# Pairs of neighbouring feature blocks, and w_in loaded by halves of its rows

## The chip, the cores and the metric

The kernel runs on one core of a Trainium2 chip. TensorE (PE in the profile) multiplies matrices, VectorE (DVE) and GpSimd (POOL) do elementwise work, ScalarE (ACT) applies functions, SyncE (SP) issues the transfers, and 16 DMA engines carry them. The metric is the time of the device from start to end in microseconds. Before the change it is 690.95 us, the median of 3 runs (690.75 to 691.02).

## The reference

Two blocks follow each other. The first is a linear attention with decay, for 4 batches and 8 heads, over 768 positions with 64 channels per head. The second takes its output as 3072 tokens of 512 features and applies two weight matrices with a leaky rectifier between them.

```python
for b in range(nb):                                   # blocks of 64 positions
    intra = einsum('bhic,bhjc->bhij', qb, kb) * Dmask
    intra = einsum('bhij,bhjd->bhid', intra, vb)
    inter = einsum('bhid,bhde->bhie', qb * lam_pow, kv_state)
    out[:, :, sl] = intra + inter
    kv_state = lam_block * kv_state + einsum('bhsd,bhse->bhde', kb * rev_pow, vb)
# ...
x = out.transpose(0, 2, 1, 3).reshape(3072, 512)
h = x @ w_in                                          # w_in: 512 x 2048
g = maximum(0.01 * h, h)
return (g @ w_out).astype(float32)                    # w_out: 2048 x 512
```

The inputs w_in and w_out are 8-byte floating-point numbers (8 bytes per element, 8 MB each), while q, k, v and the output are float32. All arithmetic on the chip is in float32.

## The kernel before

**Loading.** Each matrix of weights comes in 16 loads of 512 KB. Blocks are named (kind, p, h): kind is `wi` or `wo`, p is one of 8 pairs, h is the first or second half of the pair. The 2048 hidden features are cut in 16 blocks of 128. Before the change, pair p is made of the feature blocks p and p + 8 (`f = p + NP * h`, NP = 8):

```python
blocks = [(w, p, h) for u in range(NU) for w in ("wi", "wo") for p in range(UP * u, UP * u + UP) for h in range(2)]
# ...
def load_w(n):
    w, p, h = blocks[n]
    f = p + NP * h
    rooms[n] = room_free(n)
    # ... t is a staging room; some rooms are tiles of later weights
    def go():
        if w == "wi":
            nc.sync.dma_start(out=w_raw[n].rearrange("p (ko f) -> p ko f", ko=KO), in_=w_in_r[:, :, f * P:(f + 1) * P])
        else:
            nc.sync.dma_start(out=w_raw[n], in_=moe_w_out[f * P:(f + 1) * P, :])
```

A row of w_in is 16 KB, and a load of w_in takes 128 columns of all 512 rows: 512 pieces of 128 x 8 bytes = 1 KB. A load of w_out takes 128 whole rows of 4 KB.

**Conversion.** [...]each number is made into a float32 from its two 32-bit words. ScalarE makes the magnitude of the high word (L273), the low part (L284) and the sign (L287), for each half h. VectorE clamps (L292) and shifts (L296) the whole pair, and adds the low part for each half (L301).

```python
def dest():
    return W[p][:, 0:4:3, :] if (kind == "wi") == (h == 0) else W[p][:, 1:3, :]
def words(i, dt):
    return w_raw[n].bitcast(dt).rearrange("p (n two) -> p n two", two=2)[:, :, i].rearrange("p (a b) -> p a b", a=2)
# ...
nc.scalar.activation(out=dest(), in_=words(1, F32), func=AF.Abs)                                   # L273
nc.scalar.activation(out=addend(U16, 0), in_=words(0, U32), func=AF.Copy, bias=0.0, scale=2.0 ** -29)   # L284
nc.scalar.activation(out=addend(BF16, 1), in_=words(1, F32), func=AF.Sign, bias=tiny[:, 0:1])      # L287
# ...
nc.vector.tensor_scalar(d, d, HI_MIN, HI_MAX, op0=ALU.max, op1=ALU.min)                            # L292
nc.vector.tensor_scalar(d, d, 3, None, op0=ALU.logical_shift_left)                                 # L296
nc.vector.tensor_tensor(d, d, lo.pop(n).rearrange("p (a b) -> p a b", a=2), op=ALU.add)            # L301
```

**Seven products for eight.** Both multiplications treat their operands as 2 x 2 blocks and use seven products of sums of blocks in place of eight products of blocks. For the weights, four differences are formed per pair by three subtractions (L308), on VectorE for the pairs listed in `T_DVE` and on GpSimd for the others: a wide one gives T1 and T3 side by side, then come T2 and T4, which takes the place of B12. Pairs are counted in the order of loading (wi0, wi1, wo0, wo1, wi2, wi3, ...), so pair 3 is wo1 and pair 4 is wi2. `SI` and `SO` say at which place of a weight tile each block stands, for w_in and w_out.

```python
PROD = {"P1": ("A11", "B11"), "P2": ("A12", "B21"), "P3": ("S4", "B22"), "P4": ("A22", "T4"),
        "P5": ("S1", "T1"), "P6": ("S2", "T2"), "P7": ("S3", "T3")}
eng, e = ("DVE", nc.vector) if n // 2 in T_DVE else ("POOL", nc.gpsimd)
for o, x, y, m in (("T1", "B12", "B11", 2), ("T2", "B22", "T1", 1), ("T4", "B21", "T2", 1)):
    later[eng + " T"].append((yes, us, part(o, x, y, m), [("w", n)], (o, n)))
```

The products are issued in the order P1, P2, P6, P5, P7, P3, P4. One product is 8 matmuls of 128x128 by 128x256. There are 6 groups of tokens (GC = 4 chunks of 128 tokens each), 4 units of weights, and an `up` (L587, with w_in) and a `down` (L613, with w_out) for each. The sums S1 to S4 of the left operand are formed at L558: `xs` from the attention's output, `gS` and two more from the rectified features. The 24 chunks of the attention are done in three parts each (transposes of k and q at L370, scores and states at L354, the output at L354), placed between the products.

**The order.** A small model in the kernel's own text decides where on each engine an instruction is issued. Its settings are the string of loads (`c` is q, k and v of one chunk, `w` one load of weights), the look-ahead of the loads, `T_DVE`, and the number of attention parts beside each group of products (`STEPS`).

```python
LOADS = "cwcwcwwcwwwwcwwwcccwcwwcwwwwwwwwwwwwwwwwww" + "c" * NCH
SLACK, AHEAD = (0.7, 0), (10.0, 16.0)
T_DVE = [0, 3, 7, 9, 11, 13, 14, 15]
FIRST, STEPS = 2, [2, 2, 1, 5, 5, 6, 3, 3, 0, 0, 0, 3, 0, 1, 0, 4]
```

The transfers all stand in one queue in SyncE's order. Each waits for the transfer eight places ahead of it to have landed, besides its own room being free.

Of the kernel before, what the change touches and what calls it, by code (L numbers as in the profile page):

```python
# [38 lines left out]
F32 = mybir.dt.float32  # L39
# [5 lines left out]
ALU = mybir.AluOpType  # L45
AF = mybir.ActivationFunctionType
# [13 lines left out]
def kernel(  # L60
# [10 lines left out]
    nc = tc.nc  # L71
    P = 128
# [6 lines left out]
    KO = d_model // P  # L79
    FO = d_ff // P  # L80
    NCH = B * NCB
# [3 lines left out]
    NP = FO // 2  # L85
    HD = d_model // 2
    UP = 2
# [57 lines left out]


    QB = 2 * P
    SI = {"B11": 0, "T4": 1, "B22": 2, "B21": 3, "T1": 4, "T3": 5, "T2": 6, "B12": 1}
    SO = {"B21": 0, "B11": 1, "T4": 2, "B22": 3, "T1": 4, "T3": 5, "T2": 6, "B12": 2}
    WI, WO = [None] * NP, [None] * NP  # L150
    w_in_r = moe_w_in.rearrange("(ko ki) n -> ki ko n", ki=P)


    blocks = [(w, p, h) for u in range(NU) for w in ("wi", "wo") for p in range(UP * u, UP * u + UP) for h in range(2)]
# [2 lines left out]
    ROOMS = ["st"] + [f"{w}{p}" for w, p, h in reversed(blocks) if h == 0 and p >= UP]  # L157


    LOADS = "cwcwcwwcwwwwcwwwcccwcwwcwwwwwwwwwwwwwwwwww" + "c" * NCH  # L160
    SLACK, AHEAD = (0.7, 0), (10.0, 16.0)

    T_DVE = [0, 3, 7, 9, 11, 13, 14, 15]

    FIRST, STEPS = 2, [2, 2, 1, 5, 5, 6, 3, 3, 0, 0, 0, 3, 0, 1, 0, 4]
    rooms = {}
    w_raw, lo, w_done = {}, {}, 0

# [50 lines left out]

    def load_w(n):  # L220
        w, p, h = blocks[n]
        f = p + NP * h
        rooms[n] = room_free(n)
        pool, size = (tp, 2 * d_model) if rooms[n] == "st" else (wop, 7 * QB)
        t = pool.tile([P, size], F32, name="ws", tag=rooms[n], bufs=1)
        w_raw[n] = t[:, 0:2 * d_model].bitcast(I64)

        def go():
            if w == "wi":
                nc.sync.dma_start(out=w_raw[n].rearrange("p (ko f) -> p ko f", ko=KO), in_=w_in_r[:, :, f * P:(f + 1) * P])  # L230
            else:
                nc.sync.dma_start(out=w_raw[n], in_=moe_w_out[f * P:(f + 1) * P, :])

        run("DMA", 1.95, go, [("lowp", m) for m in range(n) if rooms[m] == rooms[n]], ("raw", n))
        ready["raw", n] += 2.0

    def room_free(n):
        later_on = {f"{w}{p}" for w, p, h in blocks[n + 1:] if (w, p) != blocks[n][:2]} | {"st"}
        return next((r for r in ROOMS if r in later_on and r not in taken()), None)

    def taken():
        return {rooms[m] for m in w_raw}
# [4 lines left out]
    def conversion(n, first):  # L247

        kind, p, h = blocks[n]
        W, s = (WI, SI) if kind == "wi" else (WO, SO)

        def dest():
            return W[p][:, 0:4:3, :] if (kind == "wi") == (h == 0) else W[p][:, 1:3, :]

        def words(i, dt):
            return w_raw[n].bitcast(dt).rearrange("p (n two) -> p n two", two=2)[:, :, i].rearrange("p (a b) -> p a b", a=2)

        def may():
            return h == 1 or n <= w_done + 2 and f"{kind}{p}" not in taken()

        def magnitude():  # L270
            if h == 0:
                W[p] = wop.tile([P, 7, QB], F32, name=f"{kind}{p}", tag=f"{kind}{p}")
            nc.scalar.activation(out=dest(), in_=words(1, F32), func=AF.Abs)  # L273

        def addend(dt, i):
            t = lo[n].rearrange("p (a b) -> p a b", a=2).bitcast(dt)
            return t.rearrange("p a (b two) -> p a b two", two=2)[:, :, :, i]

        def low_part():
            if h == 0:  # L280
                lo[n] = W[p][:, 4:6, :].rearrange("p a b -> p (a b)").bitcast(I32)
            else:
                lo[n] = tp.tile([P, d_model], I32, name="lo", tag="lo", bufs=1)
            nc.scalar.activation(out=addend(U16, 0), in_=words(0, U32), func=AF.Copy, bias=0.0, scale=2.0 ** -29)  # L284

        def sign_part():
            nc.scalar.activation(out=addend(BF16, 1), in_=words(1, F32), func=AF.Sign, bias=tiny[:, 0:1])  # L287
            del w_raw[n]

        def clamp():  # L290
            d = W[p][:, 0:4, :].rearrange("p a b -> p (a b)")
            nc.vector.tensor_scalar(d, d, HI_MIN, HI_MAX, op0=ALU.max, op1=ALU.min)  # L292

        def shift():
            d = W[p][:, 0:4, :].rearrange("p a b -> p (a b)").bitcast(I32)
            nc.vector.tensor_scalar(d, d, 3, None, op0=ALU.logical_shift_left)  # L296

        def low():
            nonlocal w_done
            d = dest().bitcast(I32)  # L300
            nc.vector.tensor_tensor(d, d, lo.pop(n).rearrange("p (a b) -> p a b", a=2), op=ALU.add)  # L301
            w_done = n + 1

        def yes():
            return True

        def part(out, a, b, m):
            return lambda: e.tensor_tensor(*(W[p][:, s[i]:s[i] + m, :] for i in (out, a, b)), op=ALU.subtract)  # L308

        later["ACT"].append((may, 0.67, magnitude, [("raw", n)], ("mag", n)))  # L310
        later["ACT"].append((lambda: h == 0 or n < w_done + 2, 0.78, low_part, [("raw", n)], ("lo", n)))
        later["ACT"].append((yes, 0.87, sign_part, [("raw", n)], ("lowp", n)))
        if h == 0:
            return low
        later["DVE"].append((yes, 0.95, clamp, [("mag", n)], ("c", n - 1)))
        later["DVE"].append((yes, 0.95, shift, [], ("s", n - 1)))
        later["DVE"].append((yes, 0.84, first, [("lowp", n - 1)], ("w", n - 1)))
        later["DVE"].append((yes, 0.84, low, [("lowp", n)], ("w", n)))
        eng, e = ("DVE", nc.vector) if n // 2 in T_DVE else ("POOL", nc.gpsimd)

        for o, x, y, m in (("T1", "B12", "B11", 2), ("T2", "B22", "T1", 1), ("T4", "B21", "T2", 1)):
            us = {"DVE": 0.15 + 0.27 * m, "POOL": 0.13 + 0.75 * m}[eng]
            later[eng + " T"].append((yes, us, part(o, x, y, m), [("w", n)], (o, n)))
# [4 lines left out]
    loaded, qT, kT, qsT, X, G, sc, po, pu = {}, {}, {}, {}, {}, {}, {}, {}, {}  # L328
# [233 lines left out]
    def operand(g, s):  # L562
        i = A.index(s)
        return X[g][:, i // 2, i % 2] if i < 4 else XS[g][:, i - 4]
# [6 lines left out]
    def up(g, u):  # L571
        q4 = ("A11", "A12", "A21", "A22")

        def begin():
            if 0 < g not in XS:
                x_sums(g)

            G[g, u] = {s: xp.tile([P, UP, T], F32, name=f"g{s}", tag=f"g{s}") for s in A[:6]}
            G[g, u].update(S3=G[g, u]["A21"], S4=G[g, u]["A12"])

        def mm(t, name, first):
            sa, sb = PROD[name]
            x = operand(g, sa)
            for i in range(UP):
                w = WI[UP * u + i][:, SI[sb], :].rearrange("p (k f) -> p k f", k=2)
                for kk in range(2):
                    nc.tensor.matmul(t[:, i, :], lhsT=w[:, kk, :], rhs=x[:, kk, :],  # L587
                                     start=(first and i == 0 and kk == 0), stop=(i == UP - 1 and kk == 1),
                                     skip_group_check=True)

        def done(i):
            if i != 2:
                leaky(G[g, u][q4[i]], G[g, u][q4[i]], f"tot{i}", q4[i])
            else:
                sums("DVE", 0.72, G[g, u], ("S1", "S2"), ["A21", "A22", "A11"])

        parts = product(mm, 1.73, lambda i: G[g, u][q4[i]], lambda z: leaky(G[g, u]["A21"], z, "Z", "A21"), done,
                        lambda name: [("sum", "POOL" if g else "DVE", PROD[name][0]), ("x", GC * g + GC - 1 - 2 * (name in ("P1", "P2")))])
        return [lambda: (begin(), parts[0]())] + parts[1:]
# [3 lines left out]
    def down(g, u):  # L603
# [5 lines left out]
        def mm(t, name, first):  # L609
            sa, sb = PROD[name]  # L610
            for m in range(T // P):
                for i in range(UP):
                    nc.tensor.matmul(t[:, m, :], lhsT=G[g, u][sa][:, i, m * P:(m + 1) * P], rhs=WO[UP * u + i][:, SO[sb], :],  # L613
                                     start=(first and m == 0 and i == 0), stop=(i == UP - 1), skip_group_check=True)
            if name == "P2":
                sums("DVE", 0.72, G[g, u], ("S3",), [])
                sums("DVE", 0.72, G[g, u], ("S4",), ["W"])
# [41 lines left out]
    for n in range(NW):  # L659
        first = conversion(n, first)  # L660
    for i, x in enumerate(LOADS):
        n = len(loads[x])
# [55 lines left out]
```

## Time and profile before

| What | Value |
|---|---|
| time, median of 3 | 690.95 us (690.75 to 691.02) |
| span of the profiled run | 689.4 us |
| TensorE busy | 672.5 us, 98% |
| VectorE, ScalarE, GpSimd busy | 330.2, 216.7, 140.4 us |
| moved by DMA | 42.81 MB in 93,146 packets |
| packets under 512 B, 512 B to 2 KB, 2 to 8 KB | 76,704; 14,336; 2,048 |
| a w_in load, issue to landing | 5.7 us (median of 16) |
| a w_out load, issue to landing | 5.3 us (median of 16) |

The page gives busy times for the whole span and then the span in 40 slices. A group of instructions is written as line, engine, operation, tile written, tiles read. In a list in order of time, the first column is the start, the second the duration of the merged row, and a bracket holds the idle time of the engine before it and what ended it. A stage line gives its length, then the busy time of TensorE, of its weight loads, of VectorE, ScalarE and GpSimd (with counts), then TensorE's granted clock, the share of the DMA engines and GB/s. Packets of 256 B are q, k and v (a row of 64 channels in float32), those of 1 KB are w_in and the output, those of 4 KB are w_out.

### The profile page before, as it was taken

How to read it: one execution, taken by the hardware profiler on the slowest of the kernel's cores; microseconds unless marked ns; L12 is line 12 of the kernel's file. 1: busy time of each engine (PE TensorE's matmuls, PEld its weight loads, DVE VectorE, ACT ScalarE, POOL GpSimd, SP SyncE). 2: the span in 40 equal slices, each digit the busy share in tenths (PEclk: the TensorE clock that was granted, in tenths of full speed). 3: DMA queues.
4: the chain of work that ended last, by engine and by line, in shares of the span. 5: the costliest groups of instructions: out<-in, count | busy, mean ns of one | idle time of the engine just before them, and what ended most of it. 6: DMA issues, size and time to landing. Idle time of an engine off the chain costs nothing.

```text
span 689.4 us, 13357 instructions
## 1 busy us (share of the span) xinstructions
PE 672.5 (98%) x5834; PEld 578.5 (84%) x5834; DVE 330.2 (48%) x496; ACT 216.7 (31%) x361; POOL 140.4 (20%) x136
## 2 busy tenths in 40 slices
PE   7789999999999999999999999999999999999997
PEld 4578887888888888888888888888888888888886
DVE  5797899982342543324426324344333244224324
ACT  4788777532222122230211321212122211221210
POOL 3546265641001032110114201204000003000000
PEclk9999999999999999999999999999999999999999
DMA  9999545623001004220210301000100000100001
GB/s 209 270 289 273 154 130 136 168 63 92 1 6 41 1 1 124 47 46 2 48 31 16 108 1 32 1 1 1 62 1 0 1 1 16 47 0 1 1 0 62
DMA packets 93146, 42.81 MB, mean 62 GB/s; under 512 B 76704, under 2 KB 91040, under 8 KB 93088
## 3 DMA queue, kind: packets, MB, share of 16 engines
q1 hardware_dynamic: 92944, 41.95, 22.9%
q8 instruction: 46, 0.75, 0.5%
q14 instruction: 12, 0.10, 0.0%
q10 hardware_dynamic: 144, 0.00, 0.0%
HBM read 35.66 MB, written 6.29 MB: 61 GB/s over the span
## 4 chain that ended last, share of the span: by engine, by line
PE 89%; DVE 5%; SPq 2%; DMA 2%; POOL 1%; issue 1%; ACT 1%; DVEq 0%
PE Z L587 24%; PE Z L613 22%; PE W L587 18%; PE W L613 17%; PE po L354 3%; PE pt L370 2%; PE ps L354 2%; DMA q<-in_q_dram 2%; DVE gS L558 1%; PE pu L354 1%; SPq L343 1%; DVE gA L558 1%; POOL wo L308 1%; DVE os L537 0%; SPq L230 0%
## 5 line engine op out<-in xcount | busy, mean ns | idle before, releaser
L613 PE MATMUL Z<-wo,gA 128*128 128x256 f32 x576 | 137.4, 381 | 0.0
L613 PEld LDWEIGHTS Z<-wo,gA 128*128 128x128 f32 x576 | 107.9, 190 | 14.8
L587 PE MATMUL Z<-xs,wi 128*128 128x256 f32 x384 | 90.9, 380 | 2.0 <-DVE xs L558 2.0
L587 PE MATMUL Z<-x,wi 128*128 128x256 f32 x384 | 92.8, 385 | 0.0
L587 PE MATMUL W<-xs,wi 128*128 128x256 f32 x384 | 92.0, 382 | 0.0
L613 PE MATMUL W<-wo,gA 128*128 128x256 f32 x384 | 91.1, 380 | 0.0
L533 ACT COPY gA<-Z 128x512 f32<-128x512 f32 x48 | 28.0, 583 | 178.6 <-PE Z L587 178.4
L587 PEld LDWEIGHTS Z<-xs,wi 128*128 128x128 f32 x384 | 72.8, 190 | 12.1 <-DVE xs L558 2.2
L587 PEld LDWEIGHTS Z<-x,wi 128*128 128x128 f32 x384 | 73.1, 192 | 10.1
L613 PEld LDWEIGHTS W<-wo,gA 128*128 128x128 f32 x384 | 72.6, 190 | 10.0
L549 ACT ACTIVATE gA<-gA 128x512 f32<-128x512 f32 x72 | 45.4, 630 | 113.2 <-DVE gA L537 113.0
L587 PEld LDWEIGHTS W<-xs,wi 128*128 128x128 f32 x384 | 71.3, 190 | 9.6
L537 DVE TENSOR_TENSOR gA<-gA,W 128x512 f32<-128x512 f32 x48 | 33.0, 687 | 83.3 <-PE W L587 83.0
L382 POOL TENSOR_TENSOR k<-k,decay 128x512 f32<-128x512 f32 (+1 forms) x24 | 28.0, 1165 | 202.9 <-PE pt L370 198.2
L537 DVE TENSOR_TENSOR gA<-gA,Z 128x512 f32<-128x512 f32 x24 | 16.5, 687 | 99.1 <-PE Z L587 99.1
L436 POOL TENSOR_TENSOR state<-state,pow_q 128x256 f32<-128x256 f32 x40 | 29.0, 725 | 119.5 <-DVE state L433 111.2
L613 PE MATMUL W<-wo,gS 128*128 128x256 f32 x192 | 46.2, 383 | 0.5 <-DVE os L537 0.5
L613 PE MATMUL Z<-wo,gS 128*128 128x256 f32 x192 | 45.7, 381 | 0.7 <-DVE os L531 0.7
L587 PE MATMUL W<-x,wi 128*128 128x256 f32 x192 | 45.6, 380 | 0.3 <-DVE os L624 0.3
L537 DVE TENSOR_TENSOR os<-os,W 128x512 f32<-128x512 f32 x48 | 32.8, 683 | 24.6 <-PE W L613 24.6
L613 PEld LDWEIGHTS W<-wo,gS 128*128 128x128 f32 x192 | 35.6, 189 | 6.9 <-DVE os L537 1.9
L613 PEld LDWEIGHTS Z<-wo,gS 128*128 128x128 f32 x192 | 36.1, 190 | 6.1 <-DVE os L531 1.2
(79 smaller groups left out, 726.9 us busy)
## 6 DMA issues: line engine op xcount, KB each, us to landing
ws<-in_moe_w_in_dram SPq DMA_DIRECT2D x16, 512.0 KB, 5.7
ws<-in_moe_w_out_dram SPq DMA_DIRECT2D x16, 512.0 KB, 5.3
k<-in_k_dram SPq DMA_DIRECT2D x48, 128.0 KB, 4.0
q<-in_q_dram SPq DMA_DIRECT2D x48, 128.0 KB, 3.0
v<-in_v_dram SPq DMA_DIRECT2D x24, 256.0 KB, 3.7
out_dram<-os SPq DMA_DIRECT2D x23, 256.0 KB, 2.2
out_dram<-os SPq DMA_DIRECT2D x2, 128.0 KB, 1.8
lam_b<-in_lam_dram ACTq DMA_DIRECT2D x1, 4.0 KB, 2.7
```

The source lines that it names most:

```text
L308: return lambda: e.tensor_tensor(*(W[p][:, s[i]:s[i] + m, :] for i in (out, a, b)), op=ALU.subtract)
L343: nc.sync.dma_start(out=x[:, i * HP:(i + 1) * HP, :], in_=y[i::2].rearrange("h p d -> p h d"))
L354: nc.tensor.matmul(out[HALF[cols]], lhsT=lhsT[HALF[rows]], rhs=rhs[HALF[rows]], start=start, stop=True, skip_group_check=True)
L370: nc.tensor.transpose(out=pt[:, y, :], in_=loaded[c][i][:, 2 * y:2 * y + 2, :].rearrange("p a d -> p (a d)"), identity=ident)
L382: run("POOL", 1.2, lambda: nc.gpsimd.tensor_tensor(kr[n], kr[n], _bc(pow_k, 3, D)[n], op=ALU.mult), [("pt", "k")], ("kd", c))
L436: run("POOL", 0.8, lambda: nc.gpsimd.tensor_tensor(state[(m + 1) % 4], new, _bc(lam_c, 2, D), op=ALU.mult), [("state", m)], ("lstate", m + 1))
L533: run("ACT", 0.6, lambda: nc.scalar.copy(dst(i), st[tag]), [tag], f"keep{i}")
L537: lambda: nc.vector.tensor_tensor(dst(i), dst(i), st[tag], op=ALU.add), [f"keep{i}", tag], f"tot{i}")
L549: run("ACT", 0.64, lambda: nc.scalar.activation(out=dst, in_=src, func=AF.Prelu, bias=0.0, scale=1.0, alpha=0.01), [after], gives)
L558: run(eng, us, lambda: e.tensor_tensor(t[o], t[a], t[b], op=op), after, ("sum", eng, o))
L587: nc.tensor.matmul(t[:, i, :], lhsT=w[:, kk, :], rhs=x[:, kk, :], start=(first and i == 0 and kk == 0), stop=(i == UP - 1 and kk == 1), sk ...
L613: nc.tensor.matmul(t[:, m, :], lhsT=G[g, u][sa][:, i, m * P:(m + 1) * P], rhs=WO[UP * u + i][:, SO[sb], :], start=(first and m == 0 and i ...
```

## The change

Pair p is now made of the neighbouring feature blocks 2p and 2p + 1. Both lie side by side in w_in, so a load takes 256 columns (2 KB pieces) of half of the rows: half h is now rows 256h to 256h + 255, in place of one feature block over all rows. Each load of w_in remains 512 KB, in 256 pieces instead of 512. For w_out, a load is still 128 whole rows, but neighbouring ones. As a half of w_in is now a half of its rows, as it is for w_out, the first half of each pair fills the same places of its tile for both kinds, and one table `SB` serves both. The string of loads, the look-ahead, `T_DVE` and `STEPS` are set anew.

```diff
-    SI = {"B11": 0, "T4": 1, "B22": 2, "B21": 3, "T1": 4, "T3": 5, "T2": 6, "B12": 1}
-    SO = {"B21": 0, "B11": 1, "T4": 2, "B22": 3, "T1": 4, "T3": 5, "T2": 6, "B12": 2}
+    SB = {"B21": 0, "B11": 1, "T4": 2, "B22": 3, "T1": 4, "T3": 5, "T2": 6, "B12": 2}
...
-    LOADS = "cwcwcwwcwwwwcwwwcccwcwwcwwwwwwwwwwwwwwwwww" + "c" * NCH
-    SLACK, AHEAD = (0.7, 0), (10.0, 16.0)
-    T_DVE = [0, 3, 7, 9, 11, 13, 14, 15]
-    FIRST, STEPS = 2, [2, 2, 1, 5, 5, 6, 3, 3, 0, 0, 0, 3, 0, 1, 0, 4]
+    LOADS = "cwcwcwwcwwwwwcwwcccwcwwcwwwwwwwwwwwwwwwwww" + "c" * NCH
+    SLACK, AHEAD = (0.7, 0), (10.0, 14.0)
+    T_DVE = [0, 4, 7, 9, 11, 13, 14, 15]
+    FIRST, STEPS = 2, [2, 2, 1, 5, 5, 6, 3, 3, 0, 1, 0, 2, 0, 1, 0, 4]
...
-                nc.sync.dma_start(out=w_raw[n].rearrange("p (ko f) -> p ko f", ko=KO), in_=w_in_r[:, :, f * P:(f + 1) * P])
+                nc.sync.dma_start(out=w_raw[n].rearrange("p (k f) -> p k f", k=2),
+                                  in_=w_in_r[:, 2 * h:2 * h + 2, p * QB:(p + 1) * QB])
             else:
-                nc.sync.dma_start(out=w_raw[n], in_=moe_w_out[f * P:(f + 1) * P, :])
+                nc.sync.dma_start(out=w_raw[n], in_=moe_w_out[p * QB + h * P:p * QB + (h + 1) * P, :])
...
-            return W[p][:, 0:4:3, :] if (kind == "wi") == (h == 0) else W[p][:, 1:3, :]
+            return W[p][:, 1:3, :] if h == 0 else W[p][:, 0:4:3, :]
...
-            return w_raw[n].bitcast(dt).rearrange("p (n two) -> p n two", two=2)[:, :, i].rearrange("p (a b) -> p a b", a=2)
+            order = "p (k a b) -> p a k b" if kind == "wi" else "p (a k b) -> p a k b"
+            return w_raw[n].bitcast(dt).rearrange("p (n two) -> p n two", two=2)[:, :, i].rearrange(order, a=2, k=2)
...
-                w = WI[UP * u + i][:, SI[sb], :].rearrange("p (k f) -> p k f", k=2)
+                w = WI[UP * u + i][:, SB[sb], :].rearrange("p (k f) -> p k f", k=2)
```

In the two programs as built, the instructions of each engine are the same in number. Their order differs in these places: the fifth w_in load stands ahead of chunk 4 instead of behind it; the three subtractions of wo1 stand on GpSimd instead of VectorE and those of wi2 the other way; ScalarE's two copies of chunk 4's transposes stand behind the conversion of wo1 instead of within it; and one part of an attention step (scores, states) stands ahead of a group of products instead of in a later one.

More of the change, by code (lines that the diff above doesn't have):

```diff
@@ L221, in load_w @@
         w, p, h = blocks[n]
-        f = p + NP * h
         rooms[n] = room_free(n)
@@ L258, in conversion @@
         kind, p, h = blocks[n]
-        W, s = (WI, SI) if kind == "wi" else (WO, SO)
+        W = WI if kind == "wi" else WO
         def dest():
-            return W[p][:, 0:4:3, :] if (kind == "wi") == (h == 0) else W[p][:, 1:3, :]
+            return W[p][:, 1:3, :] if h == 0 else W[p][:, 0:4:3, :]
         def words(i, dt):
-            return w_raw[n].bitcast(dt).rearrange("p (n two) -> p n two", two=2)[:, :, i].rearrange("p (a b) -> p a b", a=2)
+            order = "p (k a b) -> p a k b" if kind == "wi" else "p (a k b) -> p a k b"
+            return w_raw[n].bitcast(dt).rearrange("p (n two) -> p n two", two=2)[:, :, i].rearrange(order, a=2, k=2)
         def may():
@@ L272, in magnitude @@
                 W[p] = wop.tile([P, 7, QB], F32, name=f"{kind}{p}", tag=f"{kind}{p}")
-            nc.scalar.activation(out=dest(), in_=words(1, F32), func=AF.Abs)
+            nc.scalar.activation(out=dest().rearrange("p a (k b) -> p a k b", k=2), in_=words(1, F32), func=AF.Abs)
         def addend(dt, i):
-            t = lo[n].rearrange("p (a b) -> p a b", a=2).bitcast(dt)
-            return t.rearrange("p a (b two) -> p a b two", two=2)[:, :, :, i]
+            t = lo[n].bitcast(dt).rearrange("p (n two) -> p n two", two=2)[:, :, i]
+            return t.rearrange("p (a k b) -> p a k b", a=2, k=2)
         def low_part():
@@ L307, in part @@
         def part(out, a, b, m):
-            return lambda: e.tensor_tensor(*(W[p][:, s[i]:s[i] + m, :] for i in (out, a, b)), op=ALU.subtract)
+            return lambda: e.tensor_tensor(*(W[p][:, SB[i]:SB[i] + m, :] for i in (out, a, b)), op=ALU.subtract)
         later["ACT"].append((may, 0.67, magnitude, [("raw", n)], ("mag", n)))
@@ L612, in mm @@
                 for i in range(UP):
-                    nc.tensor.matmul(t[:, m, :], lhsT=G[g, u][sa][:, i, m * P:(m + 1) * P], rhs=WO[UP * u + i][:, SO[sb], :],
+                    nc.tensor.matmul(t[:, m, :], lhsT=G[g, u][sa][:, i, m * P:(m + 1) * P], rhs=WO[UP * u + i][:, SB[sb], :],
                                      start=(first and m == 0 and i == 0), stop=(i == UP - 1), skip_group_check=True)
```

## The prediction

> **What bounds the kernel now.** I read the page first (busy shares, the slices, the chain that ended last), then TensorE's instructions in order of time, then stages of a few microseconds, then VectorE and GpSimd in order of time.
>
> ```profile
> PE 672.5 (98%) x5834; PEld 578.5 (84%) x5834; DVE 330.2 (48%) x496; ACT 216.7 (31%) x361; POOL 140.4 (20%) x136
> ...
> DMA  9999545623001004220210301000100000100001
> ...
> PE 89%; DVE 5%; SPq 2%; DMA 2%; POOL 1%; issue 1%; ACT 1%; DVEq 0%
> ```
>
> TensorE is busy for 672.5 of 689.4 us and makes 89% of the chain. The DMA engines are full in the first four slices only (a slice is 17.2 us). So the change, which is about loading and converting weights, can act on the time only where TensorE idles. In its list those places are few:
>
> ```profile
> 25.06 0.44 PE L370 MATMUL pt<-ident,q 128*128 128x128 f32 x2 [1.30 <-DMA q<-in_q_dram]
> 25.34 3.42 PE L587 MATMUL Z<-x,wi 128*128 128x256 f32 x8
> ...
> 36.60 1.99 PE L587 MATMUL Z<-xs,wi 128*128 128x256 f32 x8 [1.97 <-DVE xs L558]
> 38.43 1.89 PE L587 MATMUL W<-xs,wi 128*128 128x256 f32 x8
> ```
>
> The bracket is idle time and what ended it. Up to 25.06 the gaps in this list add up to 8.5 us, the last two (1.56 us before 22.26 and the 1.30 us shown) waits for chunk 3's k and q. At 36.60 there is one of 1.97 us. After it, gaps of 0.08 us and more add up to only 2.0 us (0.16, 0.50 and 0.29 us at 116, 118 and 133 us; 0.25, 0.49 and 0.28 us at 373, 579 and 582 us), and the last product ends at 685.6, which leaves a tail of 3.8 us. From 36.60 on the kernel is a queue of products of 1.73 us each (8 matmuls, start to start).
>
> The product at 25.34 took 3.42 us where the same eight take 1.9. The stages show why, and show the DMA:
>
> ```profile
> 20.00:25.00 5.00, 2.01 (x54) 1.16 (x46) 3.94 (x7) 4.39 (x7) 3.06 (x3) 1.00 1.08 235
> ...
> 35.00:40.00 5.00, 3.40 (x16) 3.01 (x17) 4.96 (x7) 4.30 (x8) 1.94 (x2) 1.00 1.03 330
> ```
>
> ```profile
> 26.00:27.00 1.00, 1.00 (x4) 0.82 (x3) 1.00 (x3) 0.12 (x1) 0.67 (x1) 0.50 0.92 303
> ```
>
> The last three columns are granted clock, DMA share and GB/s. After the sparse stage 20 to 25 the clock is halved. The DMA engines are at a share of about 1 in all three, with 235 GB/s while most packets are 256 B (q, k, v) and 330 while most are 1 and 4 KB.
>
> **What the Trainium skill says.** Three places.
> "DMA: Bandwidth & Descriptors", section "Why small descriptors are slow (HBM only)": about three cycles of fixed cost per packet beside one cycle per 32 B. By this (an estimate from the page) two packets of 1 KB cost 70 cycles and one of 2 KB costs 67, 4% less. The trace's packet records agree in direction: 18.8 ns for 256 B, 50.1 ns for 1 KB, 193.2 ns for 4 KB on average, which is 48 to 50 ns per KB from 1 KB up, against 75 at 256 B.
> "TensorE: Matmul & The Clock Gate", section "What's actually happening": the clock is halved by recent idleness. The trace agrees (0.50 above, 3.42 us for eight matmuls against 1.9).
> "SBUF — State Buffer", section "Who interferes with whom": a VectorE instruction with two SBUF inputs, or in a two-port mode, and a GpSimd instruction block one another. The trace agrees:
>
> ```profile
> 38.87 1.76 DVE L292 TENSOR_SCALAR wo<-wo 128x1024 f32<-128x1024 f32 x1
> ...
> 47.47 0.73 DVE L292 TENSOR_SCALAR wi<-wi 128x1024 f32<-128x1024 f32 x1
> ...
> 49.90 0.69 DVE L558 TENSOR_TENSOR gS<-gS,gA 128x512 f32<-128x512 f32 x1
> ```
>
> ```profile
> 40.04 4.01 POOL L308 TENSOR_TENSOR wo<-wo 128x512 f32<-128x512 f32 x3
> ...
> 47.03 0.62 POOL L436 TENSOR_TENSOR state<-state,pow_q 128x256 f32<-128x256 f32 x1 [0.96 <-DVE state L433]
> 55.30 1.61 POOL L382 TENSOR_TENSOR k<-k,decay 64x512 f32<-64x512 f32 x1 [7.65 <-PE pt L370]
> ```
>
> The clamp (L292) takes 1.76 us beside a busy GpSimd and 0.73 beside an idle one. GpSimd is idle from 47.65 to 55.30, which the change uses.
>
> **The change, part by part.**
>
> *1. Pieces of 2 KB.* A load of w_in is 512 packets of 1 KB: 512 x 50.1 ns / 16 engines = 1.60 us of all engines. With 256 packets of 2 KB: between the 1 and 4 KB records a straight line gives 97.8 ns against 100.2, 0.04 us saved per load; the line through 256 B and 1 KB, drawn on, gives 91.8, 0.13 us. On the path lie only the loads ahead of chunk 3's q, and the string of loads puts four there (c w c w c w w c): 0.16 to 0.52 us. I take **-0.3**. Later loads have no gap of TensorE that waits for them.
>
> *2. One layout.* Magnitudes, low parts and signs still touch 512 elements per partition; the two forms (one block, or two halves apart) took 0.65 to 0.69 us for either kind before, and the add on VectorE (L301) 0.69 for either. They swap places between first and second half: **0**. Matmuls read the same shapes: **0**.
>
> *3. The string of loads.* One w_in load goes out ahead of chunk 4 instead of behind it, so chunk 4's q comes 1.6 - 0.3 = 1.3 us later. Before, TensorE took it at 33.76 and was done at 34.63; now about 35.0 to 35.9. The next product is due at 36.6 - 0.3 = 36.3. The room it loads into is free after ScalarE's conversion that ended at 22.1, before the load would go out at 24.8. So it fits into the 1.97 us gap: **0**, with 0.4 us to spare. ScalarE's copies of chunk 4 stand two places later in the new order, consistent with this.
>
> *4. Which engine forms the differences (T_DVE).* Pair 3 (wo1) goes from VectorE to GpSimd, pair 4 (wi2) the other way. VectorE loses 0.99 + 2 x 0.42 = 1.8 us between 45.6 and 50.9. GpSimd gets three subtractions behind its state update that ended at 47.65; two such took 2.40 us at 26.33, so T2 is there at 50.05 or a little earlier. The product that needs it (the third of the first down, 51.16) has 1.1 us in hand. But the clamp and shift at 47.5 then run beside GpSimd, about +0.5 us each from rows such as 1.76 and 1.11 against 0.7, and the sums gS stand behind them; these end at 50.6 today, 0.6 us ahead of need. VectorE's relief of 0.9 us ahead of the clamp pays for most: **+0.2** expected, 1.5 at worst. For wi2, VectorE has a hole of 1.50 us before 57.49 that takes 0.69 + 2 x 0.42; GpSimd's 6.91 us at 58.12 halves: **0**.
>
> *5. Steps and look-ahead.* One third of an attention step (scores, state products: 1.3 us of TensorE) is placed two groups of products earlier, at about 185 instead of 205 us. The number of switches between 64- and 128-row matmuls (0.2 us each, 1.92 against 1.73) stays. The look-ahead of 14 in place of 16 leaves the queue's order as it is. The small gaps at 116 to 133 us (0.95 us) may move, since VectorE is over 90% busy there; I take **-0.2**.
>
> *6. The halved clock.* The eight matmuls at 25.34 lose 1.5 us. If the gaps before 25.06 shrink by 0.3 us, or the window lies otherwise, it can vanish; I give this one in five: **-0.3**.
>
> Sum: -0.3 + 0.2 - 0.2 - 0.3 = -0.6, so 690.95 - 0.6 = 690.35, rounded to **690.3 us**.
>
> **Rivals.** *Hidden anyway*: chunk 3's q is paced by 256 B packets (11,264 of them at 20 ns / 16 = 14 us against 7 us for four w_in loads), and the DMA share stays at 1; then 690.9. For it: 4 KB packets are hardly cheaper per KB than 1 KB ones. *GpSimd becomes the bound of the first down*: T2 or gS late, TensorE waits 0.5 to 1.5 us at 51 us; 691.2 to 692. For it: the stretched clamp; against it: VectorE's relief. *The clock stays up*: 1.5 us gained at once, 688.8 to 689.2. For it: a clock that hangs on idleness of 2.9 us; against it: most of that idleness stays. *Chunk 4 too late*: the gap at 36.6 grows by up to 1 us; 691.3.
>
> **Range and chances.** The gain by bytes is a third of a microsecond, the clock is worth 1.5 downward, GpSimd or chunk 4 about 1 upward: 688.7 to 691.6. 2% is 13.8 us; all gaps together are 16.9, most of them untouched, so both outer chances are 0.005, and 0.99 lies within.
>
> **What would show it.** Step 1: chunk 3's q ends TensorE's wait at about 24.7 in place of 25.06, and 2 KB packets at 92 to 98 ns. Step 3: transposes of chunk 4's q before 36, no DMA named at that gap. Step 4: no idle bracket naming GpSimd or gS near 51. Step 6: the first product's time, 3.4 or 1.9. The prediction is wrong if a gap after 36.6 grows by over 1 us, or if w_in loads come much faster than 1.6 us.

## Result, and the profile after

| | before | after |
|---|---|---|
| first comparison, 4 executions each | 690.85 us (690.68 to 691.02) | 694.50 us (694.01 to 694.98) |
| ratio, with its 95% interval | | 1.0053 (1.0035 to 1.0070) |
| again, 9 executions beside 46 of before | 691.63 us (690.36 to 694.14) | 694.14 us (693.79 to 694.72) |
| ratio, with its 95% interval | | 1.0028 (1.0017 to 1.0040) |

The change made the kernel slower, by 0.28 to 0.53%. It is within 2%, as forecast, but above the range of 688.7 to 691.6 us.

The page of the kernel after, the lines that answer to those shown of before:

```profile
PE 674.7 (97%) x5834; PEld 580.5 (84%) x5834; DVE 333.1 (48%) x496; ACT 217.1 (31%) x361; POOL 139.6 (20%) x136
...
DMA  8998555533001004210201301000100000100001
...
PE 88%; DVE 6%; DMA 3%; ACT 1%; POOL 1%; issue 1%; SPq 0%; DVEq 0%
```

The shares hardly move: 3.4 us are half a percent of the span. They are found only in TensorE's instructions in order of time (start, duration, instruction, and in the bracket idle time before it and what ended it). Z and W are the accumulators that the products are written to:

```profile
23.75 0.97 PE L371 MATMUL pt<-ident,q 128*128 128x128 f32 x4
24.56 1.03 PE L588 MATMUL Z<-x,wi 128*128 128x256 f32 x4
26.72 1.13 PE L588 MATMUL Z<-x,wi 128*128 128x256 f32 x4 [1.13 <-DVE wi L302]
...
35.94 1.11 PE L371 MATMUL pt<-ident,k 128*128 128x128 f32 x4 [3.75 <-DMA k<-in_k_dram]
37.03 1.16 PE L371 MATMUL pt<-ident,q 128*128 128x128 f32 x4
37.98 2.69 PE L588 MATMUL Z<-xs,wi 128*128 128x256 f32 x8
...
59.27 1.89 PE L614 MATMUL W<-wo,gA 128*128 128x256 f32 x8
62.24 1.99 PE L614 MATMUL Z<-wo,gA 128*128 128x256 f32 x8 [1.08 <-DVE os L538]
```

Chunk 3's q needs no wait and is transposed from 23.75; in the kernel before its last two parts came at 25.06. The first product begins earlier, but its second half now waits for the conversion of wi1. Chunk 4's k is awaited for 3.75 us. The first product with xs starts 1.4 us later than before (37.98 against 36.60) and at a reduced clock. And there is a new wait of 1.08 us ahead of the last product of the first down: from 59.27 to 62.24 are 2.97 us, where a product takes 1.73, so it costs 1.24. Before, these two products stood 1.73 us apart:

```profile
57.22 1.89 PE L613 MATMUL W<-wo,gA 128*128 128x256 f32 x8
58.95 1.89 PE L613 MATMUL Z<-wo,gA 128*128 128x256 f32 x8
```

From there on both kernels run alike, 3.4 us apart. The stages of the kernel after show the slow clock after the wait (the last three columns are granted clock, DMA share, GB/s):

```profile
33.00:35.00 2.00, 0.00 (x0) 0.00 (x0) 1.93 (x5) 2.00 (x5) 0.00 (x0) 1.00 0.87 173
...
37.00:39.00 2.00, 2.00 (x8) 1.59 (x8) 2.00 (x2) 1.17 (x2) 1.43 (x2) 0.50 0.93 246
```

What stands behind the wait at 62.24 is seen in VectorE's list and in GpSimd's. The first line is of the kernel before, the others are of the kernel after:

```profile
57.49 0.69 DVE L537 TENSOR_TENSOR os<-os,Z 128x512 f32<-128x512 f32 x1 [1.50 <-PE Z L613]
...
48.67 1.65 DVE L297 TENSOR_SCALAR wi<-wi 128x1024 int32<-128x1024 int32 x1
50.24 1.22 DVE L559 TENSOR_TENSOR gS<-gA,gA 128x512 f32<-128x512 f32 x1
51.50 1.10 DVE L559 TENSOR_TENSOR gS<-gS,gA 128x512 f32<-128x512 f32 x1
...
57.88 3.70 DVE L309 TENSOR_TENSOR wi<-wi 128x512 f32<-128x512 f32 x3
61.50 0.68 DVE L538 TENSOR_TENSOR os<-os,Z 128x512 f32<-128x512 f32 x1
62.10 0.68 DVE L538 TENSOR_TENSOR os<-os,W 128x512 f32<-128x512 f32 x1
```

```profile
48.04 4.01 POOL L309 TENSOR_TENSOR wo<-wo 128x512 f32<-128x512 f32 x3
57.35 1.53 POOL L383 TENSOR_TENSOR k<-k,decay 64x512 f32<-64x512 f32 x1 [5.30 <-PE pt L371]
58.84 1.27 POOL L392 TENSOR_TENSOR qsT<-qT,pow_q 128x512 f32<-128x512 f32 x1
```

The three subtractions for wi2 (L309), moved to VectorE by the new list of pairs, take 3.70 us in place of the 1.53 that I had put down. While they last, GpSimd works on chunk 5 (57.35 to 60.11). The sum that frees the accumulator Z (`os<-os,Z`) stands behind them and starts at 61.50, so the last product cannot start before 62.2. In the kernel before, that sum had waited for its product (the bracket at 57.49). The bracket at 62.24 names VectorE's sum; the sum itself took 0.68 us as ever.

### The profile page after: what moved, and what is told of

It is laid out like the page before. It is cut to its first block, busy times and chain, and to the rows that moved or that the text cites. A ratio compares the mean times of both kernels' runs of the same rounds, so it can differ in the third digit from the quotient of the medians.

```text
span 692.8 us, 13352 instructions
## 1 busy us (share of the span) xinstructions
PE 674.7 (97%) x5834; PEld 580.5 (84%) x5834; DVE 333.1 (48%) x496; ACT 217.1 (31%) x361; POOL 139.6 (20%) x136
## 4 chain that ended last, share of the span: by engine, by line
PE 88%; DVE 6%; DMA 3%; ACT 1%; POOL 1%; issue 1%; SPq 0%; DVEq 0%
PE Z L588 23%; PE Z L614 22%; PE W L588 18%; PE W L614 16%; PE pt L371 3%; PE po L355 3%; DMA k<-in_k_dram 2%; PE ps L355 2%; PE pu L355 1%; DVE gS L559 1%; DMA ws<-in_moe_w_in_dram 1%; DVE wi L309 1%; DVE wi L302 1%; DVE gA L559 1%; DVE os L538 1%
## 5 line engine op out<-in xcount | busy, mean ns | idle before, releaser
L588 PEld LDWEIGHTS Z<-xs,wi 128*128 128x128 f32 x384 | 73.5, 192 | 10.1
```

## The experiments

Theory S: settings cost the time, the list of pairs (a wait of 1.1 us or more) and the place of the fifth w_in load. Theory L, the rival: the new layout is slower by itself, in its transfers or conversions. Single executions of the kernel before turned out to differ by up to 5.7 us (689.78 to 695.49), so all runs below have 9 to 22 executions beside 39 to 57 of before on the same chip. Ratios are to before; they are not simply those of the two medians.

**Settings of before, one or two at a time, on the kernel after.**

```diff
-    LOADS = "cwcwcwwcwwwwwcwwcccw..."      # first run, and third
+    LOADS = "cwcwcwwcwwwwcwwwcccw..."
-    T_DVE = [0, 4, 7, 9, 11, 13, 14, 15]   # second run, and third
+    T_DVE = [0, 3, 7, 9, 11, 13, 14, 15]
```

> The kernel after, with the string of loads of before alone (fifth w_in load behind chunk 4 again). Theory S (two settings cost the time): TensorE's wait of 3.75 us for chunk 4's k is gone; the first product with xs starts at about 35.2 us, where its sums are ready, instead of 37.98, and at full clock, another 0.7. 694.5 - 3.5 = about 691.0; the 1.1 us wait near 60 us stays. Theory L (the new layout is itself slower, in its transfers or conversions): chunk 4's k still comes after 35 us; 694 or more.

> The kernel after, with the list of pairs on VectorE of before alone (wo1 on VectorE, wi2 on GpSimd). Theory S: the wait of 1.08 us before the last product of the first down (62.24 us) is gone, and nothing else moves; 694.5 - 1.2 = about 693.3. Theory L: no difference, 694.5. A third possibility: wi2's subtractions on GpSimd, behind its work for chunk 5, come late for the second up, and the gain is lost there; 694.0 to 694.5.

> The kernel after, with both of these settings of before. Theory S: both gains add, 694.5 - 3.5 - 1.2 = about 689.8, faster than before by 1 us, which would then be what the layout gives. Theory L: above 693.

> The kernel before with the new pairs, 2 KB pieces and one layout alone, all settings of before (loads, look-ahead, T_DVE, steps). Theory S: 689.5 to 690.9, at or a little below before, since only chunk 3's q can come earlier (0.3 us by bytes; 1.3 us in the profile after). Theory L: 692 or more. If it differs from the run with two settings of before by over 0.5 us, the steps and the look-ahead matter too.

| run | time (us) | ratio (95%) |
|---|---|---|
| after, old loads | 693.48 | 1.0018 (1.0001 to 1.0035) |
| after, old list | 691.46 | 0.9996 (0.9984 to 1.0008) |
| after, old loads and list | 691.33 | 0.9989 (0.9975 to 1.0003) |
| before, new layout alone | 692.24 | 0.9998 (0.9984 to 1.0011) |
| before, on this chip | 691.89 | 1 |

The list of pairs is the larger part. With the old one the time is level with before whichever string of loads is used, and with the new one it is not. Theory L falls: the layout alone is level with before. The loads did much less than I expected (3.5 us), and the third run shows no gain from the layout where I had expected 1 us. TensorE's list of the run with the old list and the new loads shows that chunk 4's k is late there too, but by 1.08 us, not 3.75:

```profile
33.96 0.92 PE L371 MATMUL pt<-ident,k 128*128 128x128 f32 x4 [1.08 <-DMA k<-in_k_dram]
35.87 0.88 PE L371 MATMUL pt<-ident,q 128*128 128x128 f32 x4 [0.99 <-DMA q<-in_q_dram]
36.66 3.28 PE L588 MATMUL Z<-xs,wi 128*128 128x256 f32 x8
```

The next product starts at 36.66, as before (36.60). So the 3.75 us of the first profile belong to one execution more than to the kernel. Among the nine profiles with the new string of loads, chunk 4's k is awaited for 0 to 2.35 us in the others.

**After again, and single settings on before.**

> The kernel after, unchanged, beside the others on one chip, since single executions of the kernel before were seen to lie anywhere from 690.4 to 694.8 us. If the difference is real it stays 2 us or more above before; if the first comparison (four executions each) caught a bad draw of the start, it comes to within 1 us. In its profile: the wait for chunk 4's k (3.75 us in the first profile) may be shorter, as it was 1.08 us in the run with the old list of pairs and the same loads; the wait of 1.08 us near 60 us must be there again, since it doesn't depend on transfers.

> The kernel before, with the new list of pairs on VectorE alone (wo1 to GpSimd, wi2 to VectorE). Theory S: VectorE's subtractions of wi2 run beside GpSimd's work for chunk 5 and are held up, so the sum of the first down's W product comes late and TensorE waits 1.1 us near 59 us: before + 1.2 to 2.1 us. Rival (the gain of the old list in the layouts seen so far came from the layout's places): before + 0 to 0.3.

> The kernel before, with the new string of loads alone (fifth w_in load ahead of chunk 4, still 1 KB pieces). If the place of that load costs by its bytes: chunk 4's k and q 1.3 to 2 us later, of which the gap at 36.6 us hides most: before + 0 to 0.5. If it costs as the first profile of after says (k awaited for 3.75 us): before + 1.5 or more, with a wait for k in the trace.

After came out at 694.14 us, 1.0028 (1.0017 to 1.0040): the loss is real, and smaller than in the first comparison. Its profile has no wait for chunk 4's k, and again 1.16 us ahead of the same product. Before with the new list alone took 693.31 us, 1.0028 (1.0020 to 1.0037), with a wait of 1.09 us at 62.95 and the three subtractions at 3.72 us. Before with the new loads alone took 692.06, 1.0005 (0.9995 to 1.0015), not told apart from before. Its waits for chunk 4 (0.65 and 1.40 us) end inside the old gap: the product with xs starts at 36.60 there too.

**Which half of the swapped pair costs.** Both pairs on GpSimd, then both on VectorE:

```diff
-    T_DVE = [0, 4, 7, 9, 11, 13, 14, 15]
+    T_DVE = [0, 7, 9, 11, 13, 14, 15]         # both on GpSimd
+    T_DVE = [0, 3, 4, 7, 9, 11, 13, 14, 15]   # both on VectorE
```

> The kernel after, with both wo1 and wi2 on GpSimd. It parts two ways in which the new list can cost: if VectorE's subtractions of wi2, held up by GpSimd, are the cause, the wait near 60 us is gone and the time is that of after less 1.1 to 2 us. If wo1 on GpSimd is the cause (VectorE's clamp, shift and sums stretched near 50 us), nothing is gained. If GpSimd becomes the bound (wi2 and wi3 behind one another), a new wait shows at the third product of the second up, near 66 us, and part of the gain is lost.

> The kernel after, with both wo1 and wi2 on VectorE; GpSimd has no subtractions of weights between 44 and 60 us. If wi2 on VectorE beside chunk 5's work on GpSimd is the cause: the three subtractions of wi2 still take about 3.7 us in place of 1.5, the wait of 1.1 us near 60 us is still there, and the time stays at that of after (694.1, less up to 0.5). If wo1 on GpSimd is the cause: no wait, after less 1.1 to 2 us.

Both on GpSimd: 692.70 us, 1.0011 (0.9999 to 1.0022), which is 1.4 us less than after on the same chip. The wait near 60 us is gone, and none came at the second up. But TensorE's list shows the other half, ahead of the third product of the first down:

```profile
52.20 1.97 PE L614 MATMUL Z<-wo,gS 128*128 128x256 f32 x8 [0.60 <-DVE gS L559]
```

The shift (L297, 1.65 us) and the two sums gS (1.22 and 1.11) are stretched beside wo1's subtractions on GpSimd, as in the list of after above. In the first profile of after this was hidden: the sums ended at 52.60, and the product, late by then, came at 53.21.

Both on VectorE: 692.72, 1.0011 (1.0001 to 1.0021). The wait near 60 us is 0.30 us, less than I expected, because the program then issues one of the sums (`os<-os,Z`) after the first subtraction instead of after the third. What GpSimd does to that first subtraction is plain in VectorE's list and then GpSimd's:

```profile
55.55 2.79 DVE L309 TENSOR_TENSOR wi<-wi 128x512 f32<-128x512 f32 x1
58.27 0.68 DVE L538 TENSOR_TENSOR os<-os,Z 128x512 f32<-128x512 f32 x1
58.87 0.87 DVE L309 TENSOR_TENSOR wi<-wi 128x256 f32<-128x256 f32 x2
59.66 0.68 DVE L538 TENSOR_TENSOR os<-os,W 128x512 f32<-128x512 f32 x1
```

```profile
54.98 1.57 POOL L383 TENSOR_TENSOR k<-k,decay 64x512 f32<-64x512 f32 x1 [7.68 <-PE pt L371]
56.52 1.28 POOL L392 TENSOR_TENSOR qsT<-qT,pow_q 128x512 f32<-128x512 f32 x1
```

One subtraction of 128x512 lasts from 55.55 to 58.34, until half a microsecond after the second of two GpSimd instructions has ended (57.80). The two behind it run undisturbed, 0.87 us together.

**Chunk 5 off GpSimd.** The kernel after, with chunk 5's two multiplications on VectorE:

```diff
-        run("POOL", 1.2, lambda: nc.gpsimd.tensor_tensor(kr[n], kr[n], _bc(pow_k, 3, D)[n], op=ALU.mult),
+        eng, e, us = ("DVE", nc.vector, 0.72) if c == 5 else ("POOL", nc.gpsimd, 1.2)
+        run(eng, us, lambda: e.tensor_tensor(kr[n], kr[n], _bc(pow_k, 3, D)[n], op=ALU.mult),
...
-        eng, e, us = ("DVE", nc.vector, 0.72) if alone else ("POOL", nc.gpsimd, 1.4)
+        eng, e, us = ("DVE", nc.vector, 0.72) if alone or c == 5 else ("POOL", nc.gpsimd, 1.4)
```

> The kernel after, with chunk 5's two multiplications (k by its decay, q by its powers, 64x512 and 128x512) on VectorE instead of GpSimd, so that GpSimd is idle while VectorE subtracts for wi2. If GpSimd's holding of VectorE is the cause: the subtractions of wi2 take about 0.7, 0.4 and 0.4 us, the wait near 60 us is gone although VectorE has 1.4 us more to do, and the time is after less 1 to 1.5 us. If VectorE's own backlog is the cause: the wait stays or grows, 694 or more.

It took 692.97 us, 1.0013 (1.0005 to 1.0021), and the wait near 60 us is gone. VectorE's list:

```profile
58.45 0.69 DVE L539 TENSOR_TENSOR os<-os,Z 128x512 f32<-128x512 f32 x1 [0.28 <-PE Z L615]
59.06 1.15 DVE L309 TENSOR_TENSOR wi<-wi 128x512 f32<-128x512 f32 x2
60.18 0.69 DVE L539 TENSOR_TENSOR os<-os,W 128x512 f32<-128x512 f32 x1
```

With GpSimd idle the first two subtractions take 1.15 us and the third 0.42, 1.57 together in place of 3.70. The order moved as well (one sum stands ahead of all three subtractions, the other ahead of the third), so the durations are the evidence for GpSimd's part, and the vanished wait is the work of both.

**The clock.** In every profile without the transposes described here, TensorE's clock was halved in one or two windows before 41 us, each time elsewhere: on the first product in before (3.42 us), on the first with xs in the run with old loads and list (3.51). Most windows lasted 3.4 us, the longest 10.2 (new layout alone). To take it out of the comparison I had TensorE transpose the identity 12 times ahead of chunk 3's and of chunk 4's k, into a tile that the real transposes then overwrite. It adds 24 instructions and no result.

```diff
         def go():
+            for _ in range({3: 12, 4: 12}.get(c, 0) if nm == "k" else 0):
+                nc.tensor.transpose(out=pt[:, 0, :], in_=ident, identity=ident)
             for y in range(HP):
```

> The kernel after with the loads and the list of pairs of before, once more, as the base for the next run and to narrow its interval (0.9975 to 1.0003 in the first). Theory S: the new layout with these settings is level with before within 0.1%, since what chunk 3's q gains is taken by the wait for wi1's conversion in the middle of the first product (1.24 us in its profile).

> The run before this one, with 12 transposes of the identity, whose result is overwritten, ahead of chunk 3's and of chunk 4's transposes of k. They take about 1.3 us each time, in stretches where TensorE otherwise idles. If idleness halves the clock and the halved window (3.4 us somewhere between 17 and 41 us in every profile so far, 1.3 to 1.7 us lost) is what makes single executions differ: the window is rarer, the time is lower by 0.5 to 1.5 us and the spread of executions is smaller. Rival: the clock is halved all the same, or the transposes come when no idle time is left; then 0 to 2 us slower.

The base again: 691.89 us, 0.9995 (0.9983 to 1.0007). With the transposes: 690.65, **0.9982 (0.9973 to 0.9991)**, faster than before, and its executions lie within 1.5 us of each other (689.88 to 691.41, the base 690.41 to 692.69). The four runs with transposes that follow spread over 2.1 to 3.2 us, before on their chip over 5.0. This is the list of TensorE of the run with the base's settings and the transposes, at full clock throughout:

```profile
20.57 1.53 PE L371 MATMUL pt<-ident 128*128 128x128 f32 x12
22.49 0.96 PE L373 MATMUL pt<-ident,k 128*128 128x128 f32 x4 [0.39 <-DMA k<-in_k_dram]
...
32.05 1.53 PE L371 MATMUL pt<-ident 128*128 128x128 f32 x12
...
35.89 1.99 PE L590 MATMUL Z<-xs,wi 128*128 128x256 f32 x8 [1.44 <-DVE xs L561]
```

In this profile the transposes fill waits that were there anyway. Then all four combinations, with the same transposes:

> The kernel before, with the 12 transposes ahead of chunk 3's and chunk 4's k. If the gain of the run with old settings (0.18%) is the clock's alone: as much here, 690.3 to 690.9 with a narrower spread than before's. If the layout was needed for it (in the layout of before chunk 3's q comes later, so the idle time there is longer): no gain, 691.5.

> The new layout alone, all settings of before, with the same transposes. Against the run before this one it is the price of the layout with the clock out of play: 0 within 0.3 us if the layout is neutral, as I hold; lower by 0.5 us or more if the earlier q of chunk 3 is worth something.

> The kernel after with the same transposes. If the loss beyond the wait of 1.1 us is the clock: it comes to 1.2 to 1.5 us above the run of before with the transposes, about 692.0. If chunk 4's load order costs by itself: 2 us or more above it, with a wait for chunk 4's k in the trace.

> The kernel after with the old list of pairs and the same transposes. Against the run before this one: 1.2 to 1.4 us less, which is the list of pairs alone. Against the run with old loads, old list and transposes (690.65): what the place of the fifth w_in load costs; 0 to 0.5 us if it is mostly hidden, 1.5 or more if not.

| run, with the transposes | time (us) | ratio (95%) |
|---|---|---|
| before | 690.80 | 0.9987 (0.9979 to 0.9995) |
| before, new layout | 690.63 | 0.9988 (0.9978 to 0.9998) |
| after | 693.44 | 1.0036 (1.0023 to 1.0049) |
| after, old list | 691.04 | 0.9990 (0.9979 to 1.0000) |
| before without the transposes, on this chip | 691.45 | 1 |

The layout is neutral: 0.17 us between the first two rows, well within their intervals. The list of pairs costs 693.44 - 691.04 = 2.4 us, more than the 1.2 to 1.4 us expected. At 2.6 us above before with the transposes, this run of after lies where I had put the place of the load as the cause, and its profile has a wait of 1.08 us for chunk 4's k; but the run with the same loads and the old list is the faster one, so the larger part is the list. Its trace shows more than one wait: besides 1.16 us near 60 us there is one of 0.16 us for gS, as in the run with both on GpSimd.

```profile
51.46 1.97 PE L616 MATMUL Z<-wo,gS 128*128 128x256 f32 x8 [0.16 <-DVE gS L561]
...
60.65 1.99 PE L616 MATMUL Z<-wo,gA 128*128 128x256 f32 x8 [1.16 <-DVE os L540]
```

From the start of the first down to the end of the span it is 643.8 us (691.4 - 47.58) against 641.8 (689.6 - 47.79), so 2.0 us come after 47 us. The fifth w_in load costs about 0.4 us (691.04 against 690.63 and 690.65), within the scatter; in the profiles the product with xs starts at 36.70 and 36.80 us with the new loads, at 35.89 and 36.09 with the old. The run of after was not quite rid of the clock: its profile has a halved window at 18.4 to 21.8 us. The gain of the transposes does not need the new layout.

**Where the time lies in all 18 profiles.** From the start of the first down to that of the second up, TensorE takes 14.48 or 14.49 us with the old list and with chunk 5 on VectorE, 15.01 with both pairs on VectorE, 15.32 with both on GpSimd, and 15.82 to 16.31 with the new list (five profiles, one of them in the layout of before). So the list costs 1.3 to 1.8 us there. It is 1.3 in the three profiles in which the first product with xs ran at half clock for some or all of its time, and gS was in time; it is 1.7 and 1.8 in the two others, where the product that needs gS came 0.2 and 0.3 us late as well. That is less than the 1.7 to 2.4 us between medians; an interval such as 1.0020 to 1.0037 (1.4 to 2.6 us) covers both, and the rest is not assigned. From the second up to the end all 18 take 627.3 to 627.9 us, with old and new steps. All other differences lie ahead of the first down, which starts between 46.4 and 50.4 us. The run with chunk 5 on VectorE still takes 0.9 us more than before by its ratio, of which its first down (14.48 us) shows nothing; where they lie is open.

The steps and the look-ahead were not run alone. The two runs that have them new with loads and list old (0.9989 and 0.9995) and the layout alone (0.9998) do not tell them from nothing.

## Why the prediction was wrong

**Step 4, the list of pairs, is the step that failed.** It said +0.2 us; by the medians it is 1.7 us on before, 2.2 on after with the old loads (693.48 against 691.33) and 2.4 on after with the transposes. It looked for the danger at wo1 and found it by the right mechanism: the shift and the sums gS are stretched beside GpSimd (1.65, 1.22 and 1.10 us; the clamp, at 0.73, is not), which costs TensorE 0 to 0.3 us with the new list and 0.8 with both pairs on GpSimd. For wi2 it said "VectorE has a hole of 1.50 us before 57.49 that takes 0.69 + 2 x 0.42", and 0. By its own sum, 1.53 us, the work did not quite fit, and the hole was full of GpSimd's work: the row at 55.30 in GpSimd's list of before, which the prediction itself printed, is chunk 5's multiplication. The rule of the Trainium skill, "SBUF — State Buffer", "Who interferes with whom", was quoted for the one pair and not applied to the other. It was right there too: 3.70 us beside GpSimd, 1.57 beside an idle one. The rival named in the prediction, GpSimd in the way of the first down, had the size of the wait right (0.5 to 1.5 us; 1.08 to 1.16 measured), but I placed it at 51 us, where at most 0.3 us came with this list, the rest at 60 us; and its time, 691.2 to 692 us, was too low.

**Step 3, the string of loads.** It said 0, with 0.4 us in hand. Measured: 0.1 us on after with the old list (691.46 against 691.33), and 0.4 on before and with the transposes, too little to be told from 0; on after with the new list the ratios are 1.0028 and 1.0018, with intervals that overlap. The gap at 36.6 us hides the late chunk in most profiles, as argued; in one execution it did not, and TensorE waited 3.75 us for k. By bytes the load is 1.6 us. Why that execution was so much later is open: its DMA share falls to 0.87 while TensorE waits, so it was not bytes alone, and its slowest w_in load of the first 30 us took 10.1 us to land, against 7.5 to 8.5 in the eight other profiles with the new loads.

**Step 1, the pieces of 2 KB.** In the packet records of after, a packet of 2 KB takes 98.5 ns. The 50.1 ns of the prediction mixed w_in with the output, whose packets of 1 KB take 46.7 in after; those of w_in alone take 52.6 in before. So the like comparison is 105.2 against 98.5, 6% less and 0.11 us per load, and for the four loads ahead of chunk 3's q (54.6 and 104.1 ns) 0.3 us in all, as forecast. It is in the direction of the Trainium skill ("DMA: Bandwidth & Descriptors", "Why small descriptors are slow (HBM only)"), and does not show in the time. Chunk 3's q was indeed ready earlier, but the gain was taken by a wait that I had not named: the first product's second half waits for the conversion of wi1, in all but one of the 14 profiles with the new layout (0.17 to 2.28 us). In before that product ran at half clock, which hides such a wait. At full clock, with the transposes, its second half starts 1.2 us after the first in the layout of before and 2.3 to 2.9 us in the new one. Step 2 (0 for the layout) held in the time: 690.63 against 690.80 us.

**Step 5, steps and look-ahead.** The gain of 0.2 us did not come: with old and new steps the small gaps of 116 to 133 us and all that follows lie in the same 627.3 to 627.9 us.

**Step 6, the clock.** It treated the halved window as a feature of before that might vanish. It is in nearly every execution, at a place that changes, and goes with how executions of the same kernel differ: of 197 executions of before, those with a mean granted clock of 0.998 (69) have a median of 690.99 us, those with 0.995 (44) 692.07 and those with 0.993 (27) 693.50. The 4 executions of before in the first comparison lay at 690.7 to 691.0 us, near the low end of what later sets of 39 to 57 gave (medians 691.45 to 691.89). The median of after is 694.1 to 694.5 in both comparisons, so 0.8 us of the first one's 3.65 is a lucky draw of before. In the two profiles that were compared first, 3.4 us apart, 1.3 us are the list of pairs, 1.4 the late chunk 4 and 0.7 the slow clock on the product with xs. My range of 690.3 minus 1.6 plus 1.3 left out both that scatter and the true size of step 4.

## What to carry to other kernels

Before work is moved into idle time of VectorE, look at what GpSimd does in the same microseconds, and the other way round: an idle row is not a free one. Look first at which instruction stands behind the moved work, since what costs is the one that frees an accumulator. And where the question is one of a few tenths of a percent, take the clock of TensorE out of the comparison, or take many executions; two profiles alone would have put most of this loss on the late chunk and the clock.

## What I had not expected of the hardware

A VectorE subtraction with two inputs in SBUF, 0.69 us by itself, lasted 2.79 us: it did not get its turn between two GpSimd instructions that followed each other without a gap (54.98 to 56.55, and 56.52 to 57.80 us), and ended 0.54 us after the second. A short gap was enough elsewhere: taken one by one, GpSimd's three subtractions for wo1 in the profile of after stand at 48.04 to 49.77, 49.85 to 50.91 and 50.99 to 52.05, and one VectorE instruction ended 0.55 us after each (50.32, 51.46 and 52.60). So in these traces VectorE got through at a gap of 0.08 us, and without one it waited for the whole run.

And 24 transposes that compute nothing made the kernel faster than before: by 0.18% (0.09 to 0.27%) and 0.12% (0.02 to 0.22%) in two runs with the new layout and the old loads and list, and by 0.13% (0.05 to 0.21%) with the old layout. They hold the clock that TensorE's waits would have halved (the Trainium skill, "TensorE: Matmul & The Clock Gate", "What's actually happening", names recent idleness as the cause). Here four of the five profiles with the transposes have no halved window, while all 13 without them have one; and a mean granted clock of 0.999 or more stands in 54 of 78 executions with the transposes, against 10 of 366 without.
